# The first two x tiles of a dense-Mish kernel, loaded as two partition halves on two DMA queues

## The chip, the cores and the metric

The kernel runs on one core of one Trainium2 chip. The metric is device time in microseconds (us), the median of several runs. Loads are issued by two engines that own a DMA queue each: SyncE (SP, queue q1 in the profile) and ScalarE (ACT, queue q10).

## The reference

```python
B, S, D, F = 1, 2048, 512, 1792           # all bf16
h   = jnp.einsum("bsd,df->bsf", x, w1) + b1
sp  = jnp.log1p(jnp.exp(-jnp.abs(h))) + jnp.where(h > 0, h, 0)
act = h * jnp.tanh(sp)                    # Mish
out = jnp.einsum("bsf,fd->bsd", act, w2)
```

## The kernel before

The 2048 rows of x are taken in four blocks of 512. For each block the first product computes h transposed, 14 tiles f of 128 columns of w1, each summed over four slices k of 128 (weights w1, moving operand x transposed, `xT`). ScalarE applies Mish with the bias while it moves each tile out of PSUM into `a_sb`. The second product takes `a_sb` as weights and w2 as the moving operand, one row tile of 128 after the other; VectorE copies the result to `o_sb`, and SP stores it. All w1 and w2 stay in SBUF.

The order of the work is the order in which the program is written, one stream of instructions for each engine, with waits on semaphores put in by hand. `load` issues a transfer on the queue of the engine it is given and returns its token; `load_part` does so for slices k of w1's first 8 tiles (`OPEN` = 8), 256 KB for one k.

x tiles 0-1 (the first 256 rows, 256 KB) arrive untransposed in `x_nat`, with row 2p + j on partition p, tile j; 2 KB for a partition. `transpose_x` transposes them on TensorE (L147) by the identity, in halves of 64 partitions, and VectorE and ScalarE copy the results to `xT` (L155). x tiles 2-3 and the later blocks of x come by transposing DMAs. While the first transfers are under way TensorE runs seven matmuls on constants (`t_fill`, L105).

After that TensorE follows this order for the first block: k 0 for x tiles 0-1 and f 0 to 7 (the first four f in two steps of 128 columns, one for each tile), then k 1 and k 2 for tiles 0-1, then k 0 to 2 for tiles 2-3 (transfer `s_x23`), then k 3 for all four, and then f 8 to 13, which need the rest of w1. These are the lines L180 of the profile; the second product is L202. The end of each f's sum releases Mish for it (L163). The bias `b1` is loaded as 14 rows into `b1_nat`, which VectorE clears first (`t_bz`), and is needed only by Mish.

In the issuing order before, SP has x_nat, w1's k 1, then (after the third fill matmul) x tiles 2-3, k 3, the bias, the rest of w1, w2 and the other blocks of x. ScalarE has the load of its table, then a wait for `t_bz`, then w1's k 0 and k 2.

Of the kernel before, what the change touches and what calls it, by code (L numbers as in the profile page):

```python
# [5 lines left out]
P = 128  # L6
# [26 lines left out]
def bass_standalone__dense_activation_mish__prompt_kernel(  # L33
# [16 lines left out]
    x2, out2 = x[0], out[0]  # L50
# [6 lines left out]
    with ExitStack() as es:  # L57
        def sb(name, shape, t):
            return es.enter_context(nc.sbuf_tensor(name, shape, t))

        x_nat = sb("x_nat", [P, 2, D], BF)
# [12 lines left out]
        def sem(name):  # L74
            return es.enter_context(nc.semaphore(name))

        sp = Stream(nc.sync, None)
        pe = Stream(nc.tensor, sem("c_pe"))
        dve = Stream(nc.vector, sem("c_dve"))
        act = Stream(nc.scalar, sem("c_act"))  # L80
        pool = Stream(nc.gpsimd, sem("c_pool"))

        def load(q, dst, src, name, transpose=False):
            s = sem(name)
            (q.eng.dma_start_transpose if transpose else q.eng.dma_start)(dst, src).then_inc(s, 16)
            return (s, 16)
# [9 lines left out]
        def load_part(q, k0, k1, a, b):  # L96
            t = load_w1(q, slice(k0, k1), a, b)
            for f in range(a, b):
                for k in range(k0, k1):
                    t_w1[k, f] = t  # L100

        t_bz = dve.mark(nc.vector.memset(b1_nat[:, :], 0.0))  # L102
        c_w = nc.const_aps.tensor(1.0, [P, P], BF)
        c_m = nc.const_aps.tensor(1.0, [P, 512], BF)
        t_fill = [pe.mark(nc.tensor.matmul(ps[:, 7, 0:n], c_w, c_m[:, 0:n], start=True, stop=True)) for n in WARM]  # L105

        act.eng.preload_act_table(ACT.Mish)  # L107
        act.wait(t_bz)
        for k in (0, 2):
            load_part(act, k, k + 1, 0, OPEN)  # L110
        t_xn = load(sp, x_nat[:, :, :], x2[0:2 * P, :].rearrange("(p j) d -> p j d", p=P), "s_xn")
        load_part(sp, 1, 2, 0, OPEN)
        sp.wait(t_fill[2])
        t_x23 = load(sp, xT[:, :, 2 * P:4 * P], x2[2 * P:4 * P, :], "s_x23", True)
# [15 lines left out]
        t_id = dve.mark(nc.vector.tensor_scalar(ident[:, :], diff[:, :], 0, None, ALU.is_equal))  # L130
# [4 lines left out]

        def transpose_x():

            pe.wait(t_xn, t_id)
            H = P // 2
            for b0, eng, js, ks in ((0, dve, (0,), (0,)), (2, act, (1,), (0,)), (4, dve, (0, 1), (1,)), (6, act, (0, 1), (2, 3))):  # L140
                m = len(js)
                for i, k in enumerate(ks):
                    for n, j in enumerate(js):
                        lo = (i * m + n) * H
                        for h in (0, 1):
                            g = slice(h * H, (h + 1) * H)
                            mm = nc.tensor.matmul(ps[:, b0 + h, lo:lo + H], x_nat[g, j, k * P:(k + 1) * P], ident[g, g],  # L147
                                                  start=True, stop=True)
                eng.wait(pe.mark(mm))
                for i, k in enumerate(ks):  # L150
                    dst = xT[:, k, js[0] * P:(js[-1] + 1) * P].rearrange("p (j h t) -> p j h t", j=m, h=2)
                    src = ps[:, b0:b0 + 2, i * m * H:(i + 1) * m * H].rearrange("p h (j t) -> p j h t", j=m)
                    if m == 1:
                        dst, src = dst[:, 0], src[:, 0]
                    t = eng.mark(nc.vector.tensor_copy(dst, src) if eng is dve else act.eng.activation(dst, src, ACT.Copy))  # L155
                    for j in js:
                        t_cp[j, k] = t
                free[b0] = free[b0 + 1] = [t]
# [88 lines left out]
        def spread_b1():  # L247
# [4 lines left out]
            return dve.mark(nc.vector.tensor_copy(b1_sb[:, :], b1_T[:, 0:FT]))  # L252

        transpose_x()
        t_b1c = spread_b1()
        first(range(4), (0,), (0,))
# [47 lines left out]
```

## Time and profile before

| | |
|---|---|
| median of 3 runs | 105.26 us (105.13 to 105.57) |
| profiled execution, first to last instruction (span) | 102.9 us |
| left outside the span, median less span | 2.4 us |
| TensorE busy | 100.2 us, 97% of the span |
| VectorE busy | 13.1 us, 13% |
| ScalarE busy | 39.5 us, 38% |
| HBM read, written | 3.94 MB, 2.10 MB |

The profile has no time of the profiled execution besides its span; the runs were timed apart from it. All times in the profile's rows count from the first instruction of the span. PE stands for TensorE's matmuls and PEld for its weight loads, DVE for VectorE, ACT for ScalarE; SPq and ACTq are the sequencers that issue DMAs, and a row on them gives the time of issuing, not that of the transfer. An arrow (`<-`) in brackets names what ended the idle time ahead of the row. The rows call w1 and w2 both `w_sb`, and b1 `b_sb`.

### The profile page before, as it was taken

The page shows a single profiled execution, that of the slowest core. Times are in us where ns is not written, and L with a number is a line of the kernel's source. Part 1 is how long each engine was busy: PE and PEld are TensorE (multiplying, and loading weights), DVE is VectorE, ACT ScalarE, POOL GpSimd, SP SyncE. Part 2 cuts the span into 40 slices and gives each one's busy share as a digit, 9 for nine tenths or more (in the row PEclk, how much of TensorE's full clock was granted, in tenths as well). Part 3 has the DMA queues.
Part 4 walks back from the last instruction along what each step waited for, and adds up shares of the span by engine and source line. Part 5 has one row for each costly group of instructions (what it writes and reads, how often), then busy time and mean ns, then how long its engine had stood idle before and what let it go on. Part 6 is the DMA issues. An engine that isn't in the chain of part 4 may idle for free.

```text
span 102.9 us, 1196 instructions
## 1 busy us (share of the span) xinstructions
PE 100.2 (97%) x527; PEld 48.8 (47%) x527; DVE 13.1 (13%) x26; ACT 39.5 (38%) x61; POOL 0.4 (0%) x5
## 2 busy tenths in 40 slices
PE   6999999999999999999999999999999999999993
PEld 2697444444444444444444444444444444444472
DVE  1203000220220000022220000022201000020241
ACT  4301999000047777000017777400006777700000
POOL 1000000000000000000000000000000000000000
DMA  2999999991110000011001000001111000001112
GB/s 61 375 283 358 363 243 112 269 237 51 51 51 0 0 6 0 0 51 51 20 31 51 0 0 10 0 3 48 51 51 51 0 0 0 0 6 51 51 51 51
DMA packets 12977, 7.94 MB, mean 77 GB/s; under 512 B 7980, under 2 KB 12332, under 8 KB 12972
## 3 DMA queue, kind: packets, MB, share of 16 engines
q1 hardware_dynamic: 12540, 7.33, 27.4%
q10 hardware_dynamic: 432, 0.54, 1.5%
q8 instruction: 4, 0.07, 0.3%
q14 instruction: 1, 0.01, 0.0%
HBM read 3.94 MB, written 2.10 MB: 59 GB/s over the span
## 4 chain that ended last, share of the span: by engine, by line
PE 97%; DVE 0%; ACT 0%; issue 0%
PE ps L180 47%; PE ps L202 47%; PE ps L105 3%; DVE xT L155 0%; ACT o_sb L232 0%; PE ps L147 0%
## 5 line engine op out<-in xcount | busy, mean ns | idle before, releaser
L163 ACT ACTIVATE a_sb<-ps,b_sb 128x512 bf16<-128x512 f32 x56 | 37.1, 698 | 47.9 <-PE ps L180 47.9
L180 PE MATMUL ps<-xT,w_sb 128*128 128x512 bf16 (+2 forms) x252 | 49.1, 355 | 0.2 <-DVE xT L155 0.2
L202 PE MATMUL ps<-w_sb,a_sb 128*128 128x512 bf16 (+3 forms) x252 | 49.1, 355 | 0.0
L180 PEld LDWEIGHTS ps<-xT,w_sb 128*128 128x128 bf16 x252 | 24.2, 98 | 24.1 <-DVE xT L155 0.3
L202 PEld LDWEIGHTS ps<-w_sb,a_sb 128*128 128x128 bf16 x252 | 23.2, 98 | 25.5
L208 DVE CAST o_sb<-ps 128x512 bf16<-128x512 f32 x15 | 10.4, 692 | 79.8 <-PE ps L202 79.8
L232 ACT ACTIVATE o_sb<-ps 128x64 bf16<-128x64 f32 x1 | 0.2, 224 | 11.5 <-PE ps L202 11.5
L105 PE MATMUL ps<-const-bfloat16-1.0 128*128 128x512 bf16 (+1 forms) x7 | 2.7, 566 | 0.8 <-PEq L289 0.8
L105 PEld LDWEIGHTS ps<-const-bfloat16-1.0 128*128 128x128 bf16 x7 | 0.9, 138 | 2.1 <-issue 2.1
L155 ACT ACTIVATE xT<-ps 128x256 bf16<-128x256 f32 (+1 forms) x3 | 0.9, 347 | 1.7 <-PE ps L147 1.7
L107 ACT ACT_TABLE_LOAD x1 | 1.3, 1283 | 0.7 <-PEq L289 0.7
L250 DVE STREAM_TRANSPOSE b_T<-b_nat 32x32 bf16<-32x32 bf16 x4 | 0.8, 202 | 3.3 <-DMA b_nat<-in_b_dram 3.2
L232 DVE CAST o_sb<-ps 128x320 bf16<-128x320 f32 (+1 forms) x2 | 0.8, 392 | 1.5 <-PE ps L202 1.5
L155 DVE CAST xT<-ps 128x128 bf16<-128x128 f32 (+1 forms) x2 | 0.6, 354 | 2.4 <-PE ps L147 2.4
L147 PEld LDWEIGHTS ps<-ident,x_nat 64*128 64x128 bf16 x16 | 0.4, 118 | 0.4 <-DMA x_nat<-in_x_dram 0.4
L147 PE MATMUL ps<-ident,x_nat 64*128 64x64 bf16 x16 | 0.5, 222 | 0.0
L130 DVE TENSOR_SCALAR ident<-diff 128x128 bf16<-128x128 int32 x1 | 0.2, 227 | 0.2 <-POOL diff L128 0.2
L128 POOL IOTA diff<- 128x128 int32 x1 | 0.2, 234 | 0.4 <-POOLq L289 0.4
L102 DVE MEMSET b_nat<- 32x64 uint32 x1 | 0.1, 112 | 0.8 <-PEq L289 0.8
L252 DVE CAST b_sb<-b_T 128x14 f32<-128x14 bf16 x1 | 0.2, 176 | 0.0
L289 POOL MEMSET const-bfloat16-1.0<- 128x1 bf16 x1 | 0.1, 102 | 0.0
L289 POOL MEMSET const-uint8-127<- 128x1 uint8 x1 | 0.1, 102 | 0.0
(2 smaller groups left out, 0.2 us busy)
## 6 DMA issues: line engine op xcount, KB each, us to landing
out_dram<-o_sb SPq DMA_DIRECT2D x15, 128.0 KB, 1.7
w_sb<-in_w_dram SPq DMA_DIRECT2D x1, 1792.0 KB, 10.7
w_sb<-in_w_dram SPq DMA_DIRECT2D x1, 768.0 KB, 6.1
w_sb<-in_w_dram ACTq DMA_DIRECT2D x2, 256.0 KB, 3.7
w_sb<-in_w_dram SPq DMA_DIRECT2D x2, 256.0 KB, 3.7
x_nat<-in_x_dram SPq DMA_DIRECT2D x1, 256.0 KB, 2.6
out_dram<-o_sb SPq DMA_DIRECT2D x1, 80.0 KB, 1.6
xT<-in_x_dram SPq DMA_TRANSPOSE x4, 5.0
```

Of the source, the lines that this page charges most:

```text
L105: t_fill = [pe.mark(nc.tensor.matmul(ps[:, 7, 0:n], c_w, c_m[:, 0:n], start=True, stop=True)) for n in WARM]
L107: act.eng.preload_act_table(ACT.Mish)
L128: t_diff = pool.mark(pool.eng.iota(diff[:, :], pattern=[[1, P]], base=0, channel_multiplier=-1))
L130: t_id = dve.mark(nc.vector.tensor_scalar(ident[:, :], diff[:, :], 0, None, ALU.is_equal))
L147: mm = nc.tensor.matmul(ps[:, b0 + h, lo:lo + H], x_nat[g, j, k * P:(k + 1) * P], ident[g, g], start=True, stop=True)
L155: t = eng.mark(nc.vector.tensor_copy(dst, src) if eng is dve else act.eng.activation(dst, src, ACT.Copy))
L163: t = act.mark(act.eng.activation(a_sb[:, f, starts[s]:starts[s + 1]], ps[:, bank, 0:n], ACT.Mish, bias=b1_sb[:, f:f + 1]))
L180: return nc.tensor.matmul(ps[:, bank, lo:hi], w1_sb[:, k, f * P:(f + 1) * P], xT[:, k, starts[s] + lo:starts[s] + hi], start=first, stop=( ...
L202: return nc.tensor.matmul(ps[:, bank, 0:hi - lo], a_sb[:, f, i * P:(i + 1) * P], w2_sb[:, f, lo:hi], start=(f == 0), stop=(f == FT - 1))
L208: t = dve.mark(nc.vector.tensor_copy(o_sb[:, i, lo:hi], ps[:, bank, 0:hi - lo]))
L232: t = eng.mark(nc.vector.tensor_copy(dst, src) if eng is dve else act.eng.activation(dst, src, ACT.Copy))
L250: t = dve.mark(nc.vector.transpose(b1_T[j * SQ:(j + 1) * SQ, :], b1_nat[:, j * SQ:(j + 1) * SQ]))
```

## The change

x_nat is loaded in two transfers: partitions 0 to 63 on SP's queue, partitions 64 to 127 on ScalarE's, each ahead of everything else on its queue. ScalarE's table load comes behind its half, w1's k 0 and k 2 behind that, and no longer wait for VectorE's memset. `transpose_x` waits for both halves.

```diff
+        xv = x2[0:2 * P, :].rearrange("(p j) d -> p j d", p=P)
+        t_xn = [load(q, x_nat[h * P // 2:(h + 1) * P // 2, :, :], xv[h * P // 2:(h + 1) * P // 2], "s_xn%d" % h)
+                for h, q in enumerate((sp, act))]
         act.eng.preload_act_table(ACT.Mish)
-        act.wait(t_bz)
         for k in (0, 2):
             load_part(act, k, k + 1, 0, OPEN)
-        t_xn = load(sp, x_nat[:, :, :], x2[0:2 * P, :].rearrange("(p j) d -> p j d", p=P), "s_xn")
         load_part(sp, 1, 2, 0, OPEN)
...
-            pe.wait(t_xn, t_id)
+            pe.wait(t_id, *t_xn)
```

ScalarE's instructions at the start of the program, before (what a row waits for stands in brackets; `c_dve` is the count of VectorE's finished steps, here the memset):

```order
L107 ACT_TABLE_LOAD [waits barrier_Pool_Activation_PE_DVE_SP_release]
L85 DMA w1_sb<-in_w1_dram 128x1024 [waits c_dve]
L85 DMA w1_sb<-in_w1_dram 128x1024
L155 ACTIVATE xT<-ps 128x128 [waits c_pe]
L155 ACTIVATE xT<-ps 128x256 [waits c_pe]
L155 ACTIVATE xT<-ps 128x256
```

and now:

```order
L85 DMA x_nat<-in_x_dram 64x1024 [waits barrier_Pool_Activation_PE_DVE_SP_release]
L110 ACT_TABLE_LOAD
L85 DMA w1_sb<-in_w1_dram 128x1024 x2
L156 ACTIVATE xT<-ps 128x128 [waits c_pe]
L156 ACTIVATE xT<-ps 128x256 [waits c_pe]
L156 ACTIVATE xT<-ps 128x256
```

The half of x_nat stands ahead of the table load and of both w1 transfers, and the wait for VectorE is gone; what follows is as before.

TensorE at the start of the program, before (`s_xn` is x_nat's transfer, `s_w1_0_0` that of w1's k 0):

```order
L105 MATMUL ps<-const-bfloat16-1.0 128x256 x2
L147 MATMUL ps<-ident,x_nat 128x64 [waits c_dve,s_xn]
L147 MATMUL ps<-ident,x_nat 128x64 x15
L180 MATMUL ps<-xT,w1_sb 128x128 [waits s_w1_0_0,c_dve]
L180 MATMUL ps<-xT,w1_sb 128x128
```

and now:

```order
L105 MATMUL ps<-const-bfloat16-1.0 128x256 x2
L148 MATMUL ps<-ident,x_nat 128x64 [waits s_xn1,s_xn0,c_dve]
L148 MATMUL ps<-ident,x_nat 128x64 x15
L181 MATMUL ps<-xT,w1_sb 128x128 [waits s_w1_0_0,c_dve]
L181 MATMUL ps<-xT,w1_sb 128x128
```

Only the transposes' wait differs, by one semaphore more. On SP the first transfer is now 64 partitions instead of 128, and its order is the same.

## The prediction

> **What bounds the kernel now.** I read the chain of work that ended last first, in order of time: start in us, length, what.
>
> ```profile
> 0.77 2.72 PE ps L105 x7
> 3.49 0.19 PE ps L147 x3
> 3.68 0.02 issue
> 3.70 0.30 DVE xT L155
> 4.00 0.12 issue
> 4.13 12.32 PE ps L180 x84
> 16.45 12.09 PE ps L202 x56
> ...
> 88.97 12.17 PE ps L202 x84
> 101.14 0.02 issue
> 101.16 0.22 ACT o_sb L232
> ```
>
> From 4.13 us on TensorE (PE) never waits: from there to 101.14 the kernel is a fixed train of matmuls. The change can move only the moment at which that train starts, or tear a hole in its first piece. So the next view is the opening: the timeline of each engine up to 6 us (SPq and ACTq rows are DMA issues, with their issuing time).
>
> ```profile
> 0.73 1.28 ACT L107 ACT_TABLE_LOAD   x1 [0.73 <-PEq L289]
> 0.74 0.40 SPq L85 DMA_DIRECT2D x_nat<-in_x_dram  x1
> 0.81 0.11 DVE L102 MEMSET b_nat<- 32x64 uint32 x1 [0.81 <-PEq L289]
> 0.95 0.38 ACTq L85 DMA_DIRECT2D w_sb<-in_w_dram  x1
> 1.19 0.42 SPq L85 DMA_DIRECT2D w_sb<-in_w_dram  x1
> 1.36 0.46 ACTq L85 DMA_DIRECT2D w_sb<-in_w_dram  x1
> 2.24 1.31 SPq L85 DMA_TRANSPOSE xT<-in_x_dram  x1
> ...
> 2.86 0.15 PEld L105 LDWEIGHTS ps<-const-bfloat16-1.0 128*128 128x128 bf16 x1 [0.28 <-issue]
> 3.42 0.42 PEld L147 LDWEIGHTS ps<-ident,x_nat 64*128 64x128 bf16 x16 [0.41 <-DMA x_nat<-in_x_dram]
> 3.75 0.91 ACT L155 ACTIVATE xT<-ps 128x128 bf16<-128x128 f32 x3 [1.74 <-PE ps L147]
> 4.10 7.97 PEld L180 LDWEIGHTS ps<-xT,w_sb 128*128 128x128 bf16 x66 [0.26 <-DVE xT L155]
> 4.73 0.95 SPq L85 DMA_DIRECT2D w_sb<-in_w_dram  x2
> 5.18 0.50 SPq L85 DMA_DIRECT2D w_sb<-in_w_dram  x1
> ...
> 16.28 0.59 PE L202 MATMUL ps<-w_sb,a_sb 128*128 128x512 bf16 x2
> ```
>
> The first weight load of the transposes waits 0.41 us for x_nat; that is the only wait that the change aims at. For landings I took the DMA issues by windows that hold one transfer each; the last column is us from issue to landing.
>
> ```profile
> x_nat<-in_x_dram SPq DMA_DIRECT2D x1, 256.0 KB, 2.6
> ...
> w_sb<-in_w_dram ACTq DMA_DIRECT2D x1, 256.0 KB, 3.0
> ...
> w_sb<-in_w_dram SPq DMA_DIRECT2D x1, 256.0 KB, 3.6
> w_sb<-in_w_dram ACTq DMA_DIRECT2D x1, 256.0 KB, 4.3
> ...
> xT<-in_x_dram SPq DMA_TRANSPOSE x1, 4.4
> ...
> w_sb<-in_w_dram SPq DMA_DIRECT2D x1, 768.0 KB, 6.1
> w_sb<-in_w_dram SPq DMA_DIRECT2D x1, 1792.0 KB, 10.7
> ```
>
> Issue plus landing time: x_nat 3.34, w1 k 0 3.95, k 1 4.79, k 2 5.66, x tiles 2-3 6.64, w1's rest 4.73 + 6.1 = 10.83, w2 15.88. When does PE want each? The piece of 12.32 us holds 8 matmuls 128 columns wide, 44 of 256 and 32 of 512, 28672 columns, so 0.055 us for 128, 0.11 for 256, 0.22 for 512. From 4.13, then: k 1 at 4.13 + 8 x 0.055 + 4 x 0.11 = 5.01, k 2 at 5.89, x tiles 2-3 at 6.77, w1's rest at 6.77 + 24 x 0.11 + 8 x 0.22 = 11.17, w2 at 16.28. The margins are 0.22, 0.23, 0.13, 0.34 and 0.40 us. And k 0, at 3.95, is only 0.15 ahead of the first weight load at 4.10. The whole opening is paced by the stream of transfers, and PE follows it closely.
>
> The last view is which queue the packets belong to, in windows of that stream (queue, packets, share). q1 is SP's and q10 ScalarE's: ScalarE's two 256 KB transfers and its small last store make up the 0.54 MB that the page gives q10. The windows are 1.7 to 2.4 us (mean rate and queue), 2.4 to 2.75 (the same), 3.0 to 3.4, 3.65 to 4.05, 4.3 to 4.7 and 5.1 to 5.6.
>
> ```profile
> DMA packets 49, 0.10 MB, mean 143 GB/s; under 512 B 0, under 2 KB 0, under 8 KB 49
> q1 hardware_dynamic: 49, 0.10, 84.8%
> ...
> DMA packets 64, 0.13 MB, mean 374 GB/s; under 512 B 0, under 2 KB 0, under 8 KB 64
> q1 hardware_dynamic: 64, 0.13, 96.0%
> ...
> q10 hardware_dynamic: 75, 0.15, 100.8%
> ...
> q1 hardware_dynamic: 75, 0.15, 103.4%
> ...
> q10 hardware_dynamic: 77, 0.16, 106.7%
> ...
> q1 hardware_dynamic: 529, 0.14, 127.3%
> ```
>
> The queues do not share the stream packet by packet. The order is x_nat (q1), k 0 (q10), k 1 (q1), k 2 (q10), x tiles 2-3 (q1): one whole transfer of one queue, then one of the other. At the moment x_nat ends, k 0 and k 1 have both been issued long before (0.95 and 1.19), and q10 is served.
>
> **The change, part by part.** *The removed wait.* ScalarE's first DMA waited for VectorE's memset (0.81 + 0.11 = 0.92). It is worth at most 0.95 - 0.73 = 0.22 us of issue time, and at least nothing if the table load itself holds the queue. *The added issue.* ScalarE now issues half of x_nat first. An issue takes 0.38 to 0.46 us in these rows; I take SP's 0.40. The table load moves from 0.73 to about 1.15 and ends at 1.15 + 1.28 = 2.43; its next user is the copy at 3.75, so 1.3 us of idle ScalarE covers it; without that cover it would cost its 0.42. k 0's issue moves from 0.95 to 0.74 + 0.40 + 0.05 = 1.19 (0.05 is SP's gap between its first two issues), or up to 0.22 later if the table load holds the queue: 1.19 to 1.41. k 2 follows by 0.41, as now: 1.60 to 1.82. *SP* issues as many DMAs as before, so k 1 stays at 1.19 and everything behind it where it is. *PE* has one more semaphore to wait for: nothing if that half landed earlier, at most the 0.08 us between x_nat's landing (3.34) and the load (3.42).
>
> *x_nat itself.* The first packets of the stream cannot come earlier: SP's issue already stands at 0.74. Both halves are the same 256 KB on the same engines. If both queues fill the slow first 0.7 us (143 GB/s against 374), as much as 0.7 x (1 - 143/374) = 0.43 us could be won; if nothing overlaps, nothing. I take nothing, since the slow stretch is already 84.8% busy. The gain would be cut off anyway: k 0 lands at 3.95, so PE could start at 3.95 + 0.08 = 4.03 at best, 0.10 earlier, and x tiles 2-3 leave 0.13.
>
> *The order of the stream, which decides.* Before, x_nat was one transfer of q1, so k 0 of q10 came second. Now the first two transfers are the halves, one from each queue. If SP's half goes first, ScalarE's half is second, and the turn then falls to q1, whose next transfer is k 1. k 0 comes behind it, in the place that k 1 had: it lands at 4.79. PE needs k 0 first. Its first load would come 0.08 later, at 4.87, the first matmul 0.03 after that, at 4.90: 4.90 - 4.13 = +0.77. If ScalarE's half goes first, the turn falls to q10 and k 0 keeps its place. SP's issue stood at 0.74 and ScalarE's first instruction at 0.73, so it is close to a coin's throw; but the landing counts when the last of the 16 DMA engines is done, and one engine that takes SP's half first is enough to hold k 0 back. I take k 0 late, with ends of 0 and +0.77.
>
> Behind it nothing is late next: k 1 lands at about 3.95; k 2 at worst trades places with x tiles 2-3 and lands at 6.64, when PE, at 5.89 + 0.77 = 6.66, just wants it; the rest has 0.77 more margin than now.
>
> [...]
>
> *Sum.* The profiled span is 102.9 us, the median of the runs 105.26, so 2.4 us lie outside the first and last instruction; I keep them. Wait removed 0, issues 0, PE's semaphore 0, k 0's landing +0.77: 103.7 of span, 106.0 us.
>
> **The rivals.** *The order holds* (not slower). ScalarE's half goes first on every engine, or k 0 is served ahead of k 1 for another reason: both were queued when x_nat ended before, and the rows would look the same if the engines served by time of arrival, where k 0 (1.19 to 1.41) and k 1 (1.19) now tie. It decides as soon as k 0 lands by 4.02. Then PE starts between 4.03 and 4.21: 105.2 to 105.3.
>
> *Half rate.* Each half writes only 64 partitions. If that halves the rate, 0.13 MB take 0.69 us at 187 GB/s instead of 0.35 at 374. The first half hides in the slow start (143 GB/s, under 187 already); the second adds 0.34 to all that follows. With the old order that gives 105.6; with k 0 overtaken 106.0 + 0.34 = 106.3. No transfer of before writes 64 partitions, so no row speaks for or against it. [...]
>
> *k 0 overtaken, but cheaper.* If the stream starts faster by the 0.43 above, k 0 lands at 4.36 and costs 0.77 - 0.43 = +0.34: 105.6.
>
> **How the numbers follow.** About 0.5% (0.53 us) is what a measurement of this kernel can tell from no change. k 0 overtaken at +0.77 to +1.11: 0.50, likeliest without the half rate, 106.0, its own range 105.9 to 106.4. Order held at the old rate: 0.29. Order held at half rate, or overtaken cheaply (both +0.34): 0.17. Faster by over 0.53: no row allows it, since the margins of x tiles 2-3 and k 0 cap the gain near 0.1; 0.04 for what I do not see. So slower 0.50, same 0.29 + 0.17 = 0.46, faster 0.04. The range must hold both the held order and the overtaken one: 105.05 to 106.45, which leaves out the tails.
>
> **What would show it.** Right: the first L180 load waits for the w1 transfer of ScalarE instead of VectorE's copy, at about 4.87; in the windows q1 carries 256 KB transfers twice before q10's k 0; x_nat still lands near 3.3. Wrong: k 0 lands under 4.1 and L180 starts near 4.1. Half rate would show as a DMA rate near 190 GB/s between 2.4 and 2.9. The sum is also wrong if the longer hole (about 4.0 to 4.87) slows PE: the fill ran its matmuls at half the later pace (2.72 us for 3072 columns, against 28672 in 12.32), and the same again for 2.7 us would add about 1.4.

## The result and the profile after

The changed kernel takes 107.81 us, the median of 15 runs (105.55 to 109.67), against 105.17 us (104.38 to 105.57, 15 runs): 2.64 us or 2.5% more by medians. The ratio with its interval, 1.0123 (1.0082 to 1.0164), is taken over the five fastest runs alone (105.55 to 106.64), since a comparison leaves the slower executions out; here the spread itself comes from the change, as the experiments show, so both numbers are needed. The profiled execution has a span of 105.9 us, 3.0 more than before. A run takes 1.3 to 1.4 us more than its own span (107.25 us here), not the 2.4 us that were set outside the span: those compare one short execution, the profiled one, with the median of others. The forecast, a difference added to the median, does not change by that.

The chain of work that ended last, after:

```profile
1.38 4.10 DMA w_sb<-in_w_dram
5.48 0.14 issue
5.62 13.87 PE ps L181 x84
19.48 12.09 PE ps L203 x56
```

Two things differ, and together they are the 3.0 us. The first product starts at 5.62 instead of 4.13 (+1.49), released by the landing of w1's k 0. And its first block of 84 matmuls takes 13.87 instead of 12.32 (+1.55). Every later piece has the length it had.

The timeline of the opening, after:

```profile
0.74 0.57 ACTq L85 DMA_DIRECT2D x_nat<-in_x_dram  x1
0.74 0.56 SPq L85 DMA_DIRECT2D x_nat<-in_x_dram  x1
1.34 1.28 ACT L110 ACT_TABLE_LOAD   x1 [1.34 <-PEq L290]
1.36 0.56 SPq L85 DMA_DIRECT2D w_sb<-in_w_dram  x1
1.38 1.30 ACTq L85 DMA_DIRECT2D w_sb<-in_w_dram  x2
4.11 0.48 PEld L148 LDWEIGHTS ps<-ident,x_nat 64*128 64x128 bf16 x16 [1.10 <-issue]
5.58 6.49 PEld L181 LDWEIGHTS ps<-xT,w_sb 128*128 128x128 bf16 x50 [1.00 <-DVE xT L156]
```

The issue of a half takes 0.56 to 0.57 us where the whole took 0.40, and the transposes start at 4.11 instead of 3.42. The landings (us from issue; the two halves, then k 1 on SP, k 0 on ScalarE):

```profile
x_nat<-in_x_dram ACTq DMA_DIRECT2D x1, 128.0 KB, 3.3
x_nat<-in_x_dram SPq DMA_DIRECT2D x1, 128.0 KB, 2.6
...
w_sb<-in_w_dram SPq DMA_DIRECT2D x1, 256.0 KB, 3.3
w_sb<-in_w_dram ACTq DMA_DIRECT2D x1, 256.0 KB, 4.1
```

SP's half lands at 3.34, ScalarE's at 4.04, k 1 at 1.36 + 3.3 = 4.66, k 0 at 1.38 + 4.1 = 5.48. The queues that carry most of the packets in windows of the stream show the turns (2.7 to 2.9 us, 3.4 to 3.75, 4.3 to 4.9):

```profile
q10 hardware_dynamic: 41, 0.08, 175.9%
...
q1 hardware_dynamic: 57, 0.11, 85.8%
...
q10 hardware_dynamic: 127, 0.23, 105.0%
```

ScalarE's half on q10, then k 1 on q1, then k 0 on q10. The stream is slow in two stretches. Its rate is the last number of each row (windows of each engine's busy time), after:

```profile
1.70:2.00 0.30, 0.30 (x2) 0.03 (x1) 0.00 (x0) 0.30 (x1) 0.00 (x0) 1.00 0.00 0
...
2.90:3.40 0.50, 0.50 (x3) 0.11 (x1) 0.00 (x0) 0.00 (x0) 0.00 (x0) 1.00 0.80 135
```

and the same windows before:

```profile
1.70:2.00 0.30, 0.30 (x2) 0.03 (x1) 0.00 (x0) 0.30 (x1) 0.00 (x0) 1.00 0.65 150
...
2.90:3.40 0.50, 0.50 (x3) 0.11 (x1) 0.00 (x0) 0.00 (x0) 0.00 (x0) 1.00 1.04 389
```

Nothing moves yet at 1.7 to 2.0, and from 2.9 to 3.4 the rate is 135 GB/s instead of 389, which is 0.5 x (1 - 135/389) = 0.33 us of transfer lost.

The longer first block shows in the number of L181 matmuls in windows of one microsecond (the first x), after:

```profile
5.80:6.80 1.00, 1.00 (x10) 0.92 (x9) 1.00 1.23 297
6.80:7.80 1.00, 1.00 (x7) 0.69 (x5) 1.00 1.08 322
7.80:8.80 1.00, 1.00 (x7) 0.67 (x6) 1.00 1.01 361
9.00:10.00 1.00, 1.00 (x11) 0.90 (x10) 1.00 1.08 368
10.00:11.00 1.00, 1.00 (x12) 0.89 (x11) 1.00 1.10 349
```

TensorE is busy all the time and waits for nothing. From 6.8 to 8.8 a window counts 7 matmuls of 256 columns, from 9 on 11 to 12 of the same ones. Each window also counts the two or three that reach over its edges, so the true ratio is nearer to two: half pace for some 3.3 us (5.6 to 8.9) loses half of that, about the 1.55 us of the block. One of them ends every 0.21 us up to 8.98, and every 0.11 from there. It is the pace of the fill: the first 16 matmuls, 3072 columns, take 2.72 us, and the fill, 3072 columns as well, takes 2.72. The clock column, the third number from the end, reads 1.00 throughout, so the pace must be counted from the matmuls here; one profile below has the clock as well.

### The profile page after: what moved, and what is told of

Read it like the earlier page. It is cut to its first block, busy times and chain, and to the rows that moved or that the text cites. A ratio compares the mean times of both kernels' runs of the same rounds, so it can differ in the third digit from the quotient of the medians.

```text
span 105.9 us, 1197 instructions
## 1 busy us (share of the span) xinstructions
PE 101.9 (96%) x527; PEld 49.8 (47%) x527; DVE 13.1 (12%) x26; ACT 39.5 (37%) x61; POOL 0.4 (0%) x5
## 3 DMA queue, kind: packets, MB, share of 16 engines
HBM read 3.94 MB, written 2.10 MB: 57 GB/s over the span
## 4 chain that ended last, share of the span: by engine, by line
PE 93%; DMA 4%; ACTq 1%; ACT 0%; issue 0%
PE ps L181 47%; PE ps L203 46%; DMA w_sb<-in_w_dram 4%; ACTq L85 1%; ACT o_sb L233 0%; ACT L110 0%
## 5 line engine op out<-in xcount | busy, mean ns | idle before, releaser
L181 PE MATMUL ps<-xT,w_sb 128*128 128x512 bf16 (+2 forms) x252 | 50.6, 365 | 0.9 <-DMA w_sb<-in_w_dram 0.9
L181 PEld LDWEIGHTS ps<-xT,w_sb 128*128 128x128 bf16 x252 | 25.2, 102 | 25.5 <-DVE xT L156 1.0
```

What stands on the lines that cost most here:

```text
L181: return nc.tensor.matmul(ps[:, bank, lo:hi], w1_sb[:, k, f * P:(f + 1) * P], xT[:, k, starts[s] + lo:starts[s] + hi], start=first, stop=( ...
```

## The experiments

The theory, after these rows, has three parts: (1) with one half from each queue k 1 overtakes k 0, as forecast; (2) the halves make the stream itself late, through their shape, through two issues at one moment, or through the split over two queues; (3) idle TensorE ahead of L181 is what puts the first block at half pace. The rival of (3) is data that arrives late inside the block. A handy measure of the pace is the block's first 52 matmuls (8 of 128 columns, 44 of 256), a piece that several chains show; at full pace it takes 5.4 us.

**A hole and nothing else.** The kernel before with less fill.

```diff
-WARM = (512,) * 5 + (256,) * 2
+WARM = (512,) * 4
```

> The kernel before with the fill cut to four 512-wide matmuls, so that TensorE is idle from about 2.4 to 3.4 us; every transfer is as before. If the hole is what sets TensorE back, the first block runs at half pace for up to 3.3 us, 12.32 becomes up to 13.9, and the time is 105.2 to 106.8, spread from run to run. If late data is the reason, the time stays at 105.2.

The weight loads and the chain:

```profile
3.59 0.45 PEld L147 LDWEIGHTS ps<-ident,x_nat 64*128 64x128 bf16 x16 [1.86 <-DMA x_nat<-in_x_dram]
```

```profile
4.31 7.54 PE ps L180 x52
```

The weight loads are idle for 1.86 us ahead of the transposes instead of 0.41, and L180 starts at 4.31, 0.18 later than before. But the 52 matmuls take 7.54 us, 2.1 more (at most 1.6 was expected), and nothing is waited for inside them. 106.67 us (106.29 to 106.95) against 104.76, ratio 1.0186 (1.0135 to 1.0236). The hole is enough by itself, and in each of the four runs.

**The holes filled.** The changed kernel with fill in them.

```diff
-WARM = (512,) * 5 + (256,) * 2
+WARM = (512,) * 7 + (256,) * 2
...
         transpose_x()
+        pe.wait(*free[0])
+        for _ in range(4):
+            nc.tensor.matmul(ps[:, 0, 0:256], c_w, c_m[:, 0:256], start=True, stop=True)
```

> The changed kernel with more fill: two more 512-wide matmuls on constants ahead of the transposes, and four of 256 columns between the transposes and L181, which stand in both holes. Nothing comes earlier. If idle TensorE is why the first block runs at half pace, the piece from the first L181 to L203 is back at 12.3 us instead of 13.87, and the times draw together near 106.6 to 106.9 (105.2 + 1.5), below the changed kernel's median of 107.8. If the first block is long for another reason (data that comes late inside it), it stays near 13.9 and the time gains nothing or loses by the added work.

The chain:

```profile
4.80 0.62 PE ps L258 x4
5.42 5.25 PE ps L181 x52
```

Full pace, at about the lateness of the changed kernel. 106.06 us (105.35 to 106.52); none of the four runs lies in the tail that reached 109.67. Ratio 1.0124 (1.0064 to 1.0183): what is left fits the late start alone, 5.42 - 4.13 = 1.29 us in the profile and 106.06 - 104.76 = 1.30 by the medians. The time is below the expected 106.6 to 106.9, which started from 105.2. Theory (3) stands and its rival falls.

**The order alone.** The kernel before with k 0 and k 1 exchanged between the queues.

```diff
-        for k in (0, 2):
+        for k in (1, 2):
             load_part(act, k, k + 1, 0, OPEN)
...
-        load_part(sp, 1, 2, 0, OPEN)
+        load_part(sp, 0, 1, 0, OPEN)
```

> The kernel before with k 0 and k 1 exchanged between the queues: x_nat whole on SP, k 0 behind it on SP, k 1 and k 2 on ScalarE behind the memset's wait. Nothing is split and no issues start together; only the order of the stream changes (x_nat, k 1, k 0, k 2). Turns: k 0 lands at about 4.83 and the first L180 comes at 4.87 to 4.90, 0.77 late. Arrival: k 1, at 0.95, still ahead of k 0 at 1.19, so the same landing; this run prices the late k 0 by itself. If the hole of some 0.9 us ahead of L180 puts TensorE back to half pace, the first block takes 1 to 1.6 us more than 12.32 in some executions; if only a longer or second hole does that, it stays at 12.32 and the time is 105.9.

```profile
1.20 3.73 DMA w_sb<-in_w_dram
...
5.06 5.41 PE ps L180 x52
```

k 0 lands at 4.93, 0.10 later than expected, and L180 starts at 5.06, 0.93 late. The profiled execution kept full pace. The four runs were 105.10, 105.16, 107.42 and 107.77: two groups 2.5 us apart, as the start at full or at half pace would make them; the upper group has no profile, so that is inferred. The ratio, 1.0041 (0.9974 to 1.0107), is of the lower group and does not tell it from before.

Why did the late k 0 cost no pace in this profile? The transposes show how TensorE ran just ahead of the hole, in the changed kernel:

```profile
4.14 0.61 PE L148 MATMUL ps<-ident,x_nat 64*128 64x64 bf16 x16 [0.64 <-DMA x_nat<-in_x_dram]
```

and here:

```profile
3.65 0.41 PE L147 MATMUL ps<-ident,x_nat 64*128 64x64 bf16 x16 [0.15 <-DMA x_nat<-in_x_dram]
```

The same 16 matmuls take 0.41 us here, as in the run with the holes filled, and 0.61 us in all eight profiles whose first block begins at half pace. So in this profile full pace was reached ahead of the hole, and 1.00 us of idle TensorE behind it did not undo it; in the changed kernel the holes came before full pace. The run below with more fill in the kernel before also shows 0.61, with no long hole behind it, and its block runs at full pace.

**The wait alone.** The kernel before without `act.wait(t_bz)`.

> The kernel before without ScalarE's wait for the memset; x_nat stays whole on SP. If two issues that start at one moment slow each other, SP's x_nat and ScalarE's k 0, both at 0.74, take 0.56 instead of 0.40 us, and the stream's start and x_nat's landing move by about 0.3 (3.37 to 3.7). If the halves alone are to blame, the issues take 0.40, x_nat lands at 3.37 as before, and the time is that of before or 0.1 better.

```profile
0.74 0.40 SPq L85 DMA_DIRECT2D x_nat<-in_x_dram  x1
0.77 0.88 ACTq L85 DMA_DIRECT2D w_sb<-in_w_dram  x2
```

The queues from 2.5 to 3.2 us:

```profile
q1 hardware_dynamic: 67, 0.14, 55.5%
q10 hardware_dynamic: 61, 0.12, 45.9%
```

Two issues at one moment do not slow each other: 0.40 us, so that part of theory (2) falls. But with no 0.2 us between them the two transfers run side by side, and x_nat lands at 3.98 instead of 3.34. Neither side of the expectation had that: the wait for the memset served to let x_nat go first. The first product starts at 4.65 and the profiled block takes 14.09 us (the profiled run is one of the upper six). 106.52 us by the median of 10 runs, four of them at 104.59 to 105.16 and six at 106.49 to 107.36; ratio 1.0011 (0.9966 to 1.0057), of the lower group.

**The issues apart.** The changed kernel with ScalarE's wait ahead of its half.

```diff
+        act.wait(t_bz)
         xv = x2[0:2 * P, :].rearrange("(p j) d -> p j d", p=P)
```

> The changed kernel with ScalarE's wait for the memset put back ahead of its half of x_nat, so that the two first issues stand 0.2 us apart as before. If the simultaneous issues cost 0.31 of the stream's start, SP's issue is back at 0.40 us, and x_nat lands at about 3.5; k 0 is still overtaken by k 1 and lands near 4.9: first L181 at 5.0. If the slow-down lies in the 64 partitions, x_nat still lands near 4.0 and k 0 near 5.4.

```profile
0.74 0.57 SPq L85 DMA_DIRECT2D x_nat<-in_x_dram  x1
...
0.95 0.54 ACTq L85 DMA_DIRECT2D x_nat<-in_x_dram  x1
```

SP's issue takes 0.57 us though it stands alone. x_nat lands at 0.95 + 3.0 = 3.95 and k 0 at 1.57 + 5.1 = 6.67, more than a microsecond later than any theory had it. The profile is that of the slowest of the four runs, so k 0 need not have landed that late in the others. 106.28 us (105.65 to 108.42); the ratio, 1.0138 (1.0049 to 1.0226), is of the three lower runs.

**The same split by tile.** Two transfers on the same queues, but 128 partitions of 1 KB each.

```diff
-        t_xn = [load(q, x_nat[h * P // 2:(h + 1) * P // 2, :, :], xv[h * P // 2:(h + 1) * P // 2], "s_xn%d" % h)
+        t_xn = [load(q, x_nat[:, h, :], xv[:, h, :], "s_xn%d" % h)
```

> The changed kernel with x_nat split by tile instead of by partition: tile 0 on SP, tile 1 on ScalarE, each 128 partitions of 1 KB. Same bytes, same queues, same order of issues. If halves of 64 partitions run at half rate, the dip in the stream at 2.9 to 3.4 us goes, and x_nat lands near 3.65 instead of 4.00, k 0 at 5.1. If the dip has to do with two queues starting together, or with the start of the stream alone, x_nat lands near 4.0 and k 0 near 5.4 as in the changed kernel.

```profile
0.74 0.40 SPq L85 DMA_DIRECT2D x_nat<-in_x_dram  x1
```

```profile
0.74 0.41 ACTq L85 DMA_DIRECT2D x_nat<-in_x_dram  x1
```

The issues take 0.40 again, the stream starts before 2.0 us (116 GB/s from 1.7 to 2.0), and x_nat lands at 0.74 + 2.8 = 3.54 instead of 4.04. So 64 partitions, not the moment, cost 0.16 us an issue. In x_nat they cost 0.50 us by these two profiles, and 0.21 by the second profile of the changed kernel (below), where x_nat lands at 3.75. The second slow stretch is only smaller (242 GB/s from 2.9 to 3.4), so it does not come from the 64 partitions alone. k 0 still lands late, at 1.21 + 4.1 = 5.3, and the block takes 13.99 us: 107.19 us (106.81 to 107.61), ratio 1.0246 (1.0185 to 1.0307).

**Both halves on SP.** The kernel before, x_nat in two transfers of 64 partitions on SP.

> The kernel before with x_nat in the two halves of 64 partitions, both on SP, k 0 and k 2 on ScalarE as before. Turns: half, k 0, half, k 2, k 1, so x_nat's second half lands behind k 0, at about 4.0 instead of 3.37, and L180 starts 0.5 to 0.6 late (106); the alternation of queues in windows of the stream shows it directly. Arrival: both halves (0.74 and 1.19) against k 0 at 0.95 give the same order. If the engines ran one queue to its end, x_nat would land at 3.4 and the time stay at 105.2. Half rate: the two stretches of a half run near 190 GB/s.

The first issues, and us to landing of the second half:

```profile
0.74 1.20 SPq L85 DMA_DIRECT2D x_nat<-in_x_dram  x2
```

```profile
x_nat<-in_x_dram SPq DMA_DIRECT2D x1, 128.0 KB, 4.8
```

Two halves take 1.20 us to issue. The queues alternate as expected (from 3.0 to 3.2 us all 33 packets are q10's), so k 0 goes between the halves. The second half lands at 1.36 + 4.8 = 6.2, 2.2 later than turns alone give. 108.27 us (107.41 to 108.77), ratio 1.0332 (1.0266 to 1.0398).

**k 0 and k 1 exchanged in the changed kernel.**

```diff
-        for k in (0, 2):
+        for k in (1, 2):
             load_part(act, k, k + 1, 0, OPEN)
-        load_part(sp, 1, 2, 0, OPEN)
+        load_part(sp, 0, 1, 0, OPEN)
```

> The changed kernel with one difference: w1's k 0 is issued by SP behind its half of x_nat, and k 1 by ScalarE behind its own. If the turns between the queues set the order (halves, then q1, then q10), k 0 now takes the third place, which k 1 had: it lands near 4.63 instead of 5.48, and the first L181 comes at about 4.8 (it needs the copies too, which end at 4.7). What the two issues at one moment cost (x_nat at 4.00 instead of 3.37) stays. If engines serve by time of arrival instead, k 0 and k 1 arrive together (1.36 and 1.38) and exchanging them changes little: first L181 at 5.3 to 5.6.

```profile
x_nat<-in_x_dram ACTq DMA_DIRECT2D x1, 128.0 KB, 2.6
x_nat<-in_x_dram SPq DMA_DIRECT2D x1, 128.0 KB, 3.2
...
w_sb<-in_w_dram SPq DMA_DIRECT2D x1, 256.0 KB, 5.5
...
w_sb<-in_w_dram ACTq DMA_DIRECT2D x1, 256.0 KB, 3.1
```

This time ScalarE's half went first (3.34 against 3.94), so the turn fell to ScalarE's next transfer, k 1 (4.45), and k 0 on SP came last, at 1.37 + 5.5 = 6.87. Both expectations missed, since both took SP's half to be first; the miss shows that the first place is open when the issues stand together. 106.17 us (105.20 to 108.78); the ratio, 1.0116 (1.0027 to 1.0206), is of the three lower runs, and the profile is that of the slowest.

This profile is the only one that recorded a change of the clock that TensorE was granted. The L181 matmuls and the clock (third number from the end) in windows:

```profile
7.00:7.50 0.50, 0.48 (x9) 0.50 (x10) 1.00 1.32 361
8.00:9.00 1.00, 1.00 (x7) 0.67 (x6) 0.50 1.05 361
11.50:12.50 1.00, 1.00 (x11) 0.90 (x10) 1.00 1.10 348
```

TensorE was idle for 2.50 us ahead of L181, which starts at 7.01. It began the block at the full clock, fell to 0.50 between 7.6 and 7.7 and was back between 11.0 and 11.1, some 3.4 us later. In the same windows the matmuls of a microsecond fall to 7 and rise to 11, the two paces of the changed kernel. So the half pace of this profile is a halved clock, and it set in after the hole had ended; the other profiles show the same two paces without a record of the clock.

**The order made certain.** Stagger and exchange together, once with halves of 64 partitions, once by tile (the edits of the runs above).

> The changed kernel's halves of 64 partitions, but ScalarE's half waits for the memset, so that SP's half is always first, and k 0 (SP) and k 1 (ScalarE) are exchanged, so that k 0 has the third turn. Turns: half, half, k 0, k 1. What is left against the kernel before is the price of the 64 partitions: issues of 0.57 us instead of 0.40, x_nat at 3.9 to 4.0 instead of 3.37. First L181 at 4.7 to 4.8, and the holes ahead of it put the first block at half pace in part of the runs: 105.6 to 107.3. If 64 partitions cost nothing, L181 starts near 4.2 and the time is that of before.

> The same stagger and exchange, but x_nat is split by tile (128 partitions of 1 KB each). All three suspected costs are taken out (shape, simultaneous start, order): issues of 0.40 us, x_nat at 3.4 to 3.5, k 0 at 4.0 to 4.1, first L181 at 4.1 to 4.3, the first block at 12.3 us, and 104.7 to 105.2, the time of before. If the split over two queues costs something of its own, x_nat lands later than 3.6.

The first block, with 64 partitions:

```profile
1.36 3.77 DMA w_sb<-in_w_dram
...
5.28 7.70 PE ps L182 x52
```

and by tile:

```profile
1.20 3.28 DMA w_sb<-in_w_dram
...
4.62 5.41 PE ps L182 x52
```

With the same order, 64 partitions land x_nat at 0.95 + 2.8 = 3.75 and tiles at 0.95 + 2.3 = 3.25, and k 0 at 5.14 and 4.48: the shape costs 0.5 to 0.7 us. Both starts came later than expected: 5.28 against 4.7 to 4.8, and 4.62 against 4.1 to 4.3. In the second the queues from 3.3 to 3.7 us are mixed (46 packets of q1, 15 of q10), so k 1 already moved beside k 0. Times: 106.81 us (106.63 to 107.68), ratio 1.0209 (1.0149 to 1.0269), and 105.91 us (104.70, 104.93, 106.89, 107.30; the profile is of the first), no interval. Taking all three suspects out brought back the best runs, not the steadiness.

**More fill in the kernel before.** One matmul more in each of its two short holes.

> The kernel before with one more fill matmul of 256 columns ahead of the transposes and one of 256 behind the first copy, in the two short holes that it has (3.29 to 3.43 and 3.96 to 4.13). If short holes already cost it some pace in part of its runs (they lie between 104.2 and 105.6), the runs draw together at the lower end, 104.3 to 104.7. If its runs differ for another reason, the two matmuls only add up to 0.2 us: 104.7 to 105.0.

104.86 us (104.47 to 105.61) against 104.93, ratio 1.0012 (0.9972 to 1.0051): no gain that could be told. The kernel before is not held up by its short holes, and no version here beats it.

**The changed kernel once more.**

> The changed kernel once more, for a second profiled execution. If the queue that goes first is a matter of nanoseconds, the order of halves may differ from the first profile (SP's first) and k 0 may keep its turn; if SP is always first, k 1 lands ahead of k 0 again. If the pace of the first block is a matter of when the hole falls, this one can start at full pace (12.3 us) at the same lateness, and the span would be 1.5 us shorter.

```profile
1.39 4.54 DMA w_sb<-in_w_dram
...
6.07 8.30 PE ps L181 x52
```

SP's half was first again and k 0 last. x_nat landed at 0.75 + 3.0 = 3.75, k 1 at 1.36 + 4.4 = 5.76 and k 0 at 5.93, so only 0.17 us lie between k 1 and k 0 instead of 0.82, and both are late. The block began at half pace again; it lost 8.30 - 5.41 = 2.9 us, which is some 5.8 us at half pace. 109.05 and 110.12 us.

## Why the prediction was right or wrong

*Direction and order: right.* The turn fell to k 1, and k 0 landed 5.48 - 4.66 = 0.82 us behind it; the sum had 0.77 (or 0.84 by the places 4.79 and 3.95). The trace has sixteen landings for k 0, from 4.92 to 5.48, and L181 follows the last of them, at 5.62. The order alone cost 0.93 at the start of L180. In the second profile the order was the same, with 0.17 us between the two. That nothing behind k 0 would be late was right too: the block has no waits.

*The wait that the change aimed at: smaller than read.* The prediction took 0.41 us from the weight loads. In the chain before, the fill runs to 3.49 and the transposes follow at once, and x_nat has landed at 3.34, so hardly any time was there to win.

*"I take nothing" for x_nat itself: the first step that failed.* x_nat landed 0.70 later (4.04 against 3.34), and k 1 and k 0, in the places of k 0 and k 1 before, 0.71 and 0.69 later; x_nat was to land near 3.3. In the second profile x_nat is 0.41 late. The prediction asked how much could be won by starting both queues, 0.43 down to 0, and bounded a loss only by the halved rate. It took the issue of a half at the whole's 0.40 us; with 64 partitions it took 0.54 to 0.57, and in all seven profiles with such halves the rate from 1.7 to 2.0 us is 0, against 34 to 150 GB/s in the others. Counted in bytes, the missing start is worth 0.3 x 150/374 = 0.12 us and the stretch at 135 GB/s 0.33. That is 0.45 of the 0.7, and the rest is open.

*The half-rate rival: not what the rows show.* From 2.4 to 2.9 us the changed kernel's stream ran at 373 GB/s, as before. The halves did follow one another here, q1's (all 25 packets from 1.7 to 2.4 us) and then q10's (41 of 49 from 2.7 to 2.9), but at the full rate; the loss in these rows is in the issue and in the second slow stretch.

*The longer hole: named, and left out of the sum, the second step that failed.* The prediction put it last, at about 1.4 us, and gave it no share of the chances. It cost 1.55 in the profile (2.9 in the second), and ten of the fifteen runs lie at 107.25 us or above, where the late start alone (105.2 + 1.5 = 106.7) does not reach, not even from the slowest run of before (105.57 + 1.49 = 107.06). The other five, at 105.55 to 106.64, lie round the forecast of 106.0. That does not confirm its +0.77: the profiled start is 1.49 late, none of the five was profiled, and a start 1.49 late at full pace gives 105.87 to 107.06 from the runs of before. As far as is known, their nearness to 106.0 is luck. The nearest row was there: the fill's pace (3072 columns in 2.72 us, against 28672 in the 12.32 of the first block) shows that TensorE begins slow, and only 0.17 us separated the transposes from L180. The run with the hole alone shows that this was the term to put into the sum. How long half pace lasts is not the same everywhere: the one slow clock that was recorded lasted some 3.4 us, the changed kernel's slow stretch is 5.6 to about 8.9 us, and in its second profile it is some 5.8 us long. What sets these lengths, and why the same order is followed by full pace in some runs and half in others, no run here shows.

*The wait removed: no gain.* It was bounded by 0 to 0.22 us of gain and put at 0. With x_nat whole, the wait was what kept ScalarE's first transfer 0.2 us behind SP's, and without it x_nat lands 0.64 later. With x_nat in halves it matters little for x_nat: put back, it lands at 3.95 instead of 4.04.

*Open.* Why the stream slows a second time from 2.9 to 3.4 us. It is strong in both profiles of the changed kernel (135 and 160 GB/s) and with the issues apart (156), weaker with the holes filled (234) and when split by tile without the stagger (242), weak in the other four splits (315 to 336), and absent (385 to 406) in the four other profiles with x_nat whole. Why k 0 or a half sometimes lands over a microsecond behind its queue's turn (6.67, 6.87, 6.2) is open as well.

## What to carry to other kernels

Count the order in which the queues' transfers will be taken before splitting one: here a first transfer split over two queues gave away a turn, and the operand needed next landed behind the one needed after it, by 0.82 us (0.17 in the second profile). A wait that looks idle can be what puts one transfer first: without it x_nat, whole, landed 0.64 us later. And price a hole in TensorE's opening by the matmuls that follow it at half pace, not by its own length: here 1.5 us of lateness brought another 1.5, and in the second profile 1.9 brought 2.9. Look first whether full pace is reached ahead of the hole: with the order alone changed, it was, and 1.00 us of idle TensorE cost no pace in the profiled run.

## What was not expected of the hardware

A transfer of 64 partitions took longer to issue (0.54 to 0.57 us) than one of 128 partitions with the same bytes (0.40 and 0.41, by tile) or twice the bytes (0.40), and in the changed kernel the issue behind it on SP took 0.56 instead of 0.42. Which of two queues goes first, when their first issues stand within 0.01 us, was not fixed: SP's in both profiles of the changed kernel, ScalarE's in the one with k 0 and k 1 exchanged. In that last profile TensorE kept its full clock through 2.50 us of idleness and lost it only some 0.7 us after work had resumed.
